# Moving half a filter's rearranging copies from GpSimd to ScalarE in a fused layer-norm, long-convolution and gated-MLP kernel, under a new written-out order

## The chip, the cores and the metric

The kernel runs on one core of a Trainium2 chip. Its engines work side by side, each through its own instructions in the order in which they were written: TensorE (PE in the profile) multiplies matrices, VectorE (DVE), ScalarE (ACT) and GpSimd (POOL) work on tiles in the on-chip memory, and SyncE (SP) mostly starts DMA transfers. An engine that waits for a semaphore holds up everything behind it in its queue. The metric is the time of one execution on the device, in microseconds; lower is better.

## The reference, cut to what matters

```python
xn = layernorm(q)                                  # q: 2048 x 512, bf16
# branch A
k_shift = sum of 4 shifted copies of k, each times one column of shift_k
kv = k_shift * v
y = irfft(rfft(kv, 4096) * rfft(ssm_k, 4096))[:2048] + kv * ssm_D    # per channel
s = xn * y
# branch B: w_gate and w_up are 512 x 1792, w_down is 1792 x 512
h = gelu(xn @ w_gate) * (xn @ w_up)
g = silu(h @ w_down)
out = q + s * g
```

Branch A is a causal convolution along 2048 positions with a filter `ssm_k` (512 channels of 2048 taps each) for each channel. Branch B is a gated MLP. Both take the same normalised input.

## The kernel before, in words

The sequence of 2048 positions lies on 128 partitions with 16 positions each. It is worked in four quarters (q = 0 to 3) of 512 positions. For a quarter the MLP has 14 units (m = 0 to 13): four matmuls against `Wg`, four against `Wu` (each 128x512 out of a 128x128 weight block), a GELU on ScalarE that reads the first result out of PSUM into `GE` (L1137), and a multiplication on VectorE of the second result with `GE` into `HT` (L1140). The first two units of quarter 0 are done in halves of 256 columns (L1128, L1130). After that come the down projections against `Wd`, 14 matmuls for each of four tiles.

The convolution is a Fourier transform in two stages, written as matmuls. The shifted sum of k is made on VectorE in four groups of 2048 elements per partition: `KAC` is the running sum, `KTM` a product (L1005, L1009, L1011), and a last multiplication by v overwrites `V` (L1013). Its four columns of `shift_k` are first copied out by GpSimd into `SKB` (L986). The first stage multiplies data by the table `F1`, the results are evicted from PSUM, stored to a scratch in HBM (`ZH` for the filter, `ZK` for the data), read back in another order (`BH`, `BK`), and go through the second stage as 16 small 32x32 matmuls against `TF`. The spectra are multiplied on VectorE (`HS` and its row-swapped copy `HW`, both by `KB`), the way back uses `MI`, `ZI` and `G1`.

The filter must be transposed before its first stage, since channels lie on its partitions. It comes in four pieces `Hn[0..3]` of 128 channels (512 KB each). Pieces 0 and 1 are transposed by TensorE (L878) and copied out of PSUM into `HTr`. Pieces 2 and 3 go another way: four copies `h_perm` (tasks 58 to 61, L894), two for each piece, lay them out in `HP`, so that the taps of one residue stand together, and two transposing DMAs `h_dtr` on SP's queue (tasks 62 and 63, L899) turn `HP` into `HTD`. The first `HTD` matmuls are called the J stage (tasks `ps1J`), those of `HTr` the H stage.

Nothing is scheduled at run time. The program is a list of 788 tasks. The string `SEQ` gives the order in which they are emitted, so it gives each engine its order; a `b` behind a number picks the task's second engine. `Sched.run` goes through `SEQ` and reckons times with the costs written at each task; those costs only choose which PSUM bank and which buffer a task gets (`pF` of MLP results holds at most four banks). The constants `LOAD_NS`, `ISSUE` and `LANDS` are such reckoning too. All loads from HBM are on SP's queue in the order of `SEQ`, whatever `ORDER` says.

What a matmul of the MLP must wait for is thus: the weights' load, the transposed input `xnT`, and the bank, which is free when the GELU or the multiplication that read its last content is done.

Of the kernel before, what the change touches and what calls it, by code (L numbers as in the profile page):

```python
# [16 lines left out]
NT = 16  # L17
# [7 lines left out]
N_WARM = 11  # L25
ORDER = "x01 h0 x11 h1 x22 w0 w1 h2 h3 D0 w2 s0 k0 v0 x1 w3 k1 v1 d0 d1 k2 v2 k3 v3 x2 x3"
SEQ = (
    "0 2 17 19 5 18 21 1 3 8 4 9 10 11 6 22 12 13 7 66 67 68 74 51 50 69 75 83 53 87 70 76 103 77 71 23 20 24 72 73 84 88 37 113 108 78 118 109 "
    "378 79 380 379 80 81 381 85 104 370 86 55 89 90 371 372 54 56 14 390 392 15 373 119 25 458 32 456 29 459 382 457 30 384 33 114 57 454 398 "
    "374 28 383 460 31 35 455 385 376 391 394 461 462 34 52 396 393 16 395 400 399 149 375 26 147 464 397 120 115 116 148 466 40 463 38 401 402 "  # L30
    "377 110 64 150 406 465 404 468 39 470 407 27 60 117 121 403 151 111 405 410 386 36 469 82 408 152 58 409 473 387 388 153 414 472 474 105 412 "
    "467 122 389 47 59 430 106 422 415 154 62 416 471 411 159 417 61 155 63 44 100 413 432 156 42 43 426 94 107 112 101 41 427 428 423 429 157 "
    "424 475 431 91 425 95 477 499 92 433 93 160 158 161 97 476 96 418 503 420 504 98 505 478 500 162 231 506 163 501 226 232 227 491 185 102 502 "
    "419 507 228 233 99 508 509 234 519 229 521 144 164 421 165 65 515 123 493 46 124 167 510 520 479 45 168 145 444 135 445 522 517 129 169 166 "
    "481 170 146 138 136 446 130 480 235 241 171 141 482 139 483 447 172 175 125 173 176 137 434 242 140 142 236 132 449 230 450 237 126 174 133 "
    "177 238 178 485 127 239 451 243 131 143 448 184 484 134 246 244 435 183 248 247 128 240 48 251 179 180 181 249 436 245 439 182 437 440 49 "
    "253 252 254 441 486 452 487 261 442 438 489 516 262 453 263 443 250 643 264 488 256 644 492 186 255 258 191 511 257 259 518 495 645 187 265 "
    "490 647 497 512 494 513 496 641 188 642 260 527 196 648 266 523 646 649 551 189 190 279 498 652 514 650 653 192 651 206 529 524 193 552 194 "
    "528 531 197 530 292 536 198b 525 532 546 199 267 547 555 654 557 558 556 201 553 526 268 537 271b 533 280 541 284 281 554 559 542 269 270 "
    "272 273 548 534 560 293 538 563 297 561 543 562 539 544 294b 549 200 274 535 663 540 195 664 564 277b 545 278 550 675 665 666 677 683 295 "  # L40
    "275 685 276 655 684 296 657 282 703 676 686 202 678 283 671 298 285 659 299 331 656 673 305 203 658 204 211 286 705 661 660 662 318 672 609 "
    "287 288b 290 610 597 300 611 674 599 598 301b 612 303 593 306 310b 595 581 307 205 600 304 582 569 583 207 308 302 208 584 216 601 309 594 "
    "209 596 617 571 319 311 320b 704 706 619 602 291 323 570 212 603 213 312 618 604 214 572 210 585 586 587 725 313 289 357 577 620 314 215 "
    "316b 717 613 321 332 578 344 579 615 221 691 336b 333 317 580 315 614 217 693 692 322 218 616 219 565 324 566 325 588 326 567 220 568 667 "
    "327b 668 329 694 334 335 669 345 699 349 346 687 573 701 222 670 337 347 348 689 575 223 328 589 224 688 574 330 605 350 338 690 225 351 607 "
    "358 606 700 576 362b 679 359 339 591 608 707 702 590 342 340b 352 709 360 361 341 621 631 592 353 622 343 355 363 364 681 356 365 721 680 "
    "354 713 632 633 636 366 367 637 368b 682 369 638 719 626 627 723 639 634 715 635 623 640 624 628 695 720 629 748 625 724 755 733 731 630 722 "
    "716 727 726 697 782 696 708 711 718 749 710 698 728 732 750 735 751 729 730 778 734 712 741 786 738 714 756 776 742 736 777 784 743 737 739 "
    "744 780 745 752 746 787 757 785 758 779 781 762 763 753 754 764 747 769 765 740 770 783 759 760 761 766 767 771 772 773 768 774 775 "
)  # L50
NF_BANKS = 4
ISSUE = 470.0
LOAD_NS = {("x0_", 262144): 1200.0, ("x0_", 131072): 450.0, 262144: 900.0, 524288: 1350.0, ("x", 524288): 2100.0, ("h", 524288): 1300.0, ("wg", 524288): 1550.0, ("wu", 524288): 1450.0, 917504: 2620.0, ("sk", 524288): 1500.0, 344064: 1250.0, 46080: 350.0, 3072: 100.0, 1024: 200.0}
W_XT, W_SW, W_BK, W_BH, W_ZI, W_BI, W_ZK, W_MI, W_G1 = 1665000, 600000, 555000, 703000, 333000, 640000, 490000, 740000, 222000
NC_PAIRS = 4
SMALL = 1.15 * 262144
# [235 lines left out]
class Sched:  # L292
# [8 lines left out]
    FIRST = {"loads": 1050.0, "SP": 30500.0}  # L301
    DRAIN = 121.0
    EARLY, TAKEN, SHARED, WAIT = (0.0, 1.0), 1400.0, 46000.0, 3300.0
    LANDS = ()

    def __init__(self):
        self.tasks = []
# [37 lines left out]
    def run(self):  # L345
# [5 lines left out]
        for name in SEQ.split():  # L351
# [13 lines left out]
            if eng == "loads":  # L365
                free[eng] = t.start + dur * (self.EARLY[1] if t.start < self.EARLY[0] else 1.0)
                if n_loads < len(self.LANDS):
                    free[eng] = self.LANDS[n_loads] - self.LOAD_LAT
                n_loads += 1
# [21 lines left out]
def act(n, sb=False):  # L391
    return 170.0 + n * 0.833 + (30.0 if sb else 0.0)


def dve(n, rate):
    return 150.0 + n / 0.96 / rate


def build_kernel(nc, A_q, A_k, A_v, A_shift_k, A_ssm_k, A_ssm_D, B_w_gate, B_w_up, B_w_down, out):
    with ExitStack() as es0:  # L400
# [8 lines left out]
        def at(name, shape, dt, offset):  # L409
            return nc.alloc_sbuf_tensor_at(name, shape, dt, offset=offset)  # L410
# [46 lines left out]
        Hn = at("Hn", [128, KD, S_LEN], BF16, g_at)  # L457
        HTr = at("HTr", [128, NT // 2, DM], BF16, kk_at - 16384)
        HP = at("HP", [128, NT, 2, 128], BF16, kk_at - 8192)
# [45 lines left out]
        S = Sched()  # L505
        res = trk.res

        def dsem(name):
            return DSem(nc.alloc_semaphore(name), name)
# [79 lines left out]
        def dma(eng, out_ap, in_ap, sem, r, w):  # L589
            trk.dma(eng, lambda e: e.dma_start(out=out_ap, in_=in_ap), sem, r=r, w=w)  # L590
# [3 lines left out]
        def load(name, out_ap, in_ap, w_res, w_buf, nbytes, ring="SP", r=(), rb=()):  # L594
            sem = dsem("d_" + name)
            ns = LOAD_NS.get((name.rstrip("0123456789"), nbytes)) or LOAD_NS[nbytes]
            last_load[0] = S.add([("loads", ns)], lambda e: dma(ring, out_ap, in_ap, sem, r, w_res), r=rb, w=w_buf, nbytes=nbytes)

        def op(engs, fn, r=(), w=(), rr=(), ww=(), lat=0.0, after=()):

            def emit(e):
                R = rr() if callable(rr) else rr
                W = ww() if callable(ww) else ww
                trk.op(e, lambda h: fn(e, h), r=R, w=W)
            return S.add(engs, emit, r=r, w=w, lat=lat, after=after)

        def copy(e, h, o, i, scale=1.0):
            if e == "ACT":
                return h.activation(o, i, ACTF.Copy, scale=scale)  # L609
            if scale != 1.0:  # L610
                return h.tensor_scalar(o, i, scale, None, ALU.mult)
            return h.tensor_copy(o, i)  # L612
# [21 lines left out]
        bHP, bHTD = [[B(f"{x}{h}") for h in range(2)] for x in ("HP", "HTD")]  # L634
# [255 lines left out]
        h_perm, h_dtr = [], []  # L890
        d_htd = [dsem(f"d_htd{hf}") for hf in range(2)]
        for hf in range(2):
            for k in range(2):
                h_perm.append(op([("POOL", 1250.0)], lambda e, h, hf=hf, k=k: h.tensor_copy(HP[:, 8 * hf:8 * hf + 8, k, :], Hn[:, 2 + k, :].rearrange("p (a t) -> p t a", t=NT)[:, 8 * hf:8 * hf + 8, :]),  # L894
                                 r=[bHn[2 + k]], w=[bHP[hf]], rr=[R_Hn[2 + k]], ww=[R_HP[hf]]))
        for hf in range(2):
            def dtr(e, hf=hf):
                o = HTD[:, 8 * hf:8 * hf + 8, :, :].rearrange("p t k d -> p (t k) d")
                trk.dma("SP", lambda h: h.dma_start(out=o, in_=HP[:, 8 * hf:8 * hf + 8, :, :].rearrange("p t k a -> p (t k a)"), transpose=True), d_htd[hf], r=[R_HP[hf]], w=[R_HTD[hf]])  # L899
            h_dtr.append(S.add([("loads", 4500.0)], dtr, r=[bHP[hf]], w=[bHTD[hf]], nbytes=W_XT))  # L900
        HT0 = HTr[0:1, 0, :].rearrange("p (d c) -> p c d", c=2)[:, 0, :]
        HD0 = HTD[0:1, 0, :, :].rearrange("p k d -> p (k d)")
        bFold, bFoldD = B("fold"), B("foldD")
# [1 line left out]
           r=[bHD, *[bHTr[k][0] for k in range(2)]], w=[bFold], rr=[R_D, *R_HTr[0]], ww=R_HTr[0])  # L905
        op([("DVE", 420.0)], lambda e, h: h.tensor_tensor(HD0, HD0, Drow[:, 256:512], ALU.add),
           r=[bHD, bHTD[0]], w=[bFoldD], rr=[R_D, R_HTD[0]], ww=[R_HTD[0]])
# [284 lines left out]
        for j in range(8):  # L1192
            p = B(f"psy{j}", pC)
# [29 lines left out]
        for j in range(6):  # L1223
            d_out.append(dsem(f"d_out{j}"))
            g = G[:, 2 * j:2 * j + 2, :].rearrange("p t d -> p (t d)")
            x = X[:, 2 * j:2 * j + 2, :].rearrange("p t d -> p (t d)")
# [4 lines left out]
                  r=[b2], w=[B(f"out{j}")], nbytes=262144)  # L1231
# [55 lines left out]
```

## Time and profile before

| | us |
|---|---|
| median of 3 runs | 201.49 |
| lowest, highest | 201.22, 202.07 |
| the profiled execution, on the device | 202.13 |
| its span, first to last instruction | 200.3 |
| PE busy | 190.8 |
| DVE busy | 165.8 |
| ACT busy | 119.2 |
| POOL busy | 24.5 |

The profiled execution lies 0.64 us above the median of the runs, and 1.83 us of it lie outside the span. Matmuls overlap in the array, and their ends are modelled, so "PE busy" tells when there was a matmul under way, not that the array worked at its full rate; the rate is seen from the distance of one matmul to the next, 0.219 us for one of 512 columns at full clock (49 of them in 10.74 us). DVE instructions overlap as well: the next one starts some 0.07 us ahead of the listed end of the last.

### The profile page before, as it was taken

What the parts mean: (1) busy time and instruction counts of PE and PEld (TensorE: products, weight loads), DVE (VectorE), ACT (ScalarE), POOL (GpSimd) and SP (SyncE); (2) the same over time, 40 slices, a digit from 0 to 9 for tenths busy, and PEclk for the clock granted to TensorE, in tenths of its full rate; (3) what the DMA queues carried; (4) which work ended last, traced back from release to release, by engine and by line L of the source; (5) the groups of instructions that cost most, each with busy time, mean ns of one, the idle gap of its engine ahead of it and who ended that gap; (6) DMA issues with size and microseconds to landing.
All of it is one profiled execution on the core that took longest, in us unless ns stands there. A gap on an engine that the chain in (4) does not pass through costs nothing.

```text
span 200.3 us, 3498 instructions
## 1 busy us (share of the span) xinstructions
PE 190.8 (95%) x1365; PEld 85.7 (43%) x1377; DVE 165.8 (83%) x244; ACT 119.2 (60%) x167; POOL 24.5 (12%) x36
## 2 busy tenths in 40 slices
PE   8899988499999999999999999999999999999994
PEld 2575543134444444443434443333434334444442
DVE  7699799969988999866978787887989793288994
ACT  5787993236688786987345666677668562340121
POOL 5502699100000000020030000000000000000000
PEclk9999999669999999999999999999999999999999
DMA  5999997999967869998999993387922235866374
GB/s 172 321 340 341 387 407 225 208 253 330 252 203 253 279 164 264 411 380 238 363 154 337 252 315 127 106 279 243 318 112 105 108 124 193 303 218 211 105 265 157
DMA packets 46102, 49.19 MB, mean 246 GB/s; under 512 B 12803, under 2 KB 39943, under 8 KB 46086
## 3 DMA queue, kind: packets, MB, share of 16 engines
q1 hardware_dynamic: 37510, 42.67, 69.0%
q10 hardware_dynamic: 8576, 6.29, 9.8%
q8 instruction: 11, 0.18, 0.4%
q14 instruction: 5, 0.04, 0.1%
HBM read 27.39 MB, written 14.68 MB: 210 GB/s over the span
## 4 chain that ended last, share of the span: by engine, by line
PE 79%; DVE 7%; SPq 5%; DMA 4%; issue 3%; ACT 0%; DVEq 0%
PE psall L618 74%; SPq L590 5%; PE psall L1028 5%; DMA KK<-in_A_k_dram 4%; DVE KAC L1005 2%; DVE KTM L1009 2%; DVE KAC L1011 1%; DVE HT L1140 1%; DVE G L1175 0%; DVE G L1174 0%; ACT G L1172 0%; DVE HTr L904 0%; DVE HT L1130 0%; DVE XN L835 0%; DVEq L173 0%
## 5 line engine op out<-in xcount | busy, mean ns | idle before, releaser
L618 PE MATMUL psall<-xnT,Wu 128*128 128x512 bf16 (+1 forms) x232 | 57.5, 382 | 0.0
L618 PE MATMUL psall<-xnT,Wg 128*128 128x512 bf16 (+1 forms) x232 | 56.5, 377 | 0.0
L618 PE MATMUL psall<-Wd,HT 128*128 128x512 bf16 (+2 forms) x229 | 50.9, 366 | 0.7 <-issue 0.3
L1140 DVE TENSOR_TENSOR HT<-psall,GE 128x512 bf16<-128x512 f32 x54 | 36.6, 683 | 10.5 <-PE psall L618 10.2
L1137 ACT ACTIVATE GE<-psall 128x512 bf16<-128x512 f32 x54 | 31.5, 602 | 23.1 <-PE psall L618 14.6
L618 PEld LDWEIGHTS psall<-xnT,Wu 128*128 128x128 bf16 x232 | 22.3, 100 | 27.2 <-issue 5.0
L618 PEld LDWEIGHTS psall<-Wd,HT 128*128 128x128 bf16 x238 | 22.4, 98 | 26.0 <-issue 1.3
L618 PEld LDWEIGHTS psall<-xnT,Wg 128*128 128x128 bf16 x232 | 22.0, 99 | 26.4 <-issue 3.2
L1009 DVE TENSOR_TENSOR KTM<-KK,SKB 128x2048 bf16<-128x2048 bf16 x12 | 17.6, 1470 | 0.1
L609 ACT ACTIVATE HS<-psall 128x1024 bf16<-128x1024 f32 x15 | 14.6, 1030 | 3.0 <-PE psall L1028 3.0
L609 ACT ACTIVATE X<-psall 128x1024 bf16<-128x1024 f32 (+1 forms) x17 | 13.8, 825 | 4.2 <-PE psall L618 4.2
L1011 DVE TENSOR_TENSOR KAC<-KAC,KTM 128x2048 bf16<-128x2048 bf16 x12 | 15.8, 1320 | 0.1
L609 ACT ACTIVATE AST<-psall 128x1024 bf16<-128x1024 f32 x12 | 12.1, 1022 | 3.8 <-PE psall L618 3.8
L609 ACT ACTIVATE KB<-psall 128x1024 bf16<-128x1024 f32 x10 | 10.0, 1020 | 6.7 <-PE psall L1028 6.7
L1166 DVE SCALAR_TENSOR_TENSOR G<-G,psall 128x512 bf16<-128x512 bf16 x12 | 7.8, 681 | 7.1 <-ACT G L1164 7.1
L609 ACT ACTIVATE BO<-psall 128x1024 bf16<-128x1024 f32 x9 | 9.1, 1023 | 6.9 <-PE psall L1028 6.9
L1172 ACT ACTIVATE G<-psall 128x512 bf16<-128x512 f32 (+2 forms) x5 | 2.6, 512 | 16.6 <-PE psall L618 16.6
L612 DVE CAST BO<-psall 128x1024 bf16<-128x1024 f32 x7 | 8.6, 1223 | 4.5 <-PE psall L1028 4.5
L1164 ACT ACTIVATE G<-psall 128x512 bf16<-128x512 f32 x12 | 6.8, 597 | 8.5 <-PE psall L618 8.4
L821 DVE BATCH_NORM_STATS2 stats<-X 128x6 f32<-128x512 bf16 x16 | 10.6, 676 | 1.2 <-DMA X<-in_A_q_dram 1.2
L1091 DVE TENSOR_TENSOR HW<-KB,HW 128x1024 bf16<-128x1024 bf16 x16 | 10.9, 682 | 0.0
L831 POOL TENSOR_SCALAR mv<-mv 128x1 f32<-128x1 f32 (+1 forms) x7 | 2.0, 281 | 72.6 <-DVE mv L822 72.6
(82 smaller groups left out, 189.3 us busy)
## 6 DMA issues: line engine op xcount, KB each, us to landing
BH<-ZH SPq DMA_DIRECT2D x8, 512.0 KB, 5.2
BK<-ZK SPq DMA_DIRECT2D x8, 512.0 KB, 6.1
HW<-HS SPq DMA_DIRECT2D x16, 256.0 KB, 3.0
ZI<-BO ACTq DMA_DIRECT2D x16, 256.0 KB, 2.5
BI<-ZI SPq DMA_DIRECT2D x8, 512.0 KB, 4.3
ZK<-AST SPq DMA_DIRECT2D x6, 512.0 KB, 3.7
Hn<-in_A_ssm_k_dram SPq DMA_DIRECT2D x4, 512.0 KB, 8.4
KK<-in_A_k_dram SPq DMA_DIRECT2D x4, 512.0 KB, 9.6
```

The lines of the kernel that those rows point to most:

```text
L590: trk.dma(eng, lambda e: e.dma_start(out=out_ap, in_=in_ap), sem, r=r, w=w)
L609: return h.activation(o, i, ACTF.Copy, scale=scale)
L612: return h.tensor_copy(o, i)
L618: return h.matmul(o, lhsT=l, rhs=r, start=st, stop=sp)
L821: t_stats[t] = op([("DVE", 670.0)], lambda e, h, t=t: h.bn_stats(stats[:, t, :], X[:, t, :]), r=[bX[q][t % 4]], w=[bst[t]], rr=[R_X[t]], w ...
L1009: op([("DVE", dur)], lambda e, h, j=j, m=m: h.tensor_tensor(KTM[:, m.slot, :, :], kk(j), sk(j), ALU.mult), r=need + [bSKB[j], a], w=[m], r ...
L1011: op([("DVE", dur)], lambda e, h, m=m: h.tensor_tensor(KAC[:, a.slot, :, :], KAC[:, a.slot, :, :], KTM[:, m.slot, :, :], ALU.add), r=[m], ...
L1028: trk.op("PE", lambda h: h.matmul(ps(s, i)[b, :], lhsT=wt(col)[a, :], rhs=data(col)[a, :], start=n < 16, stop=n >= len(todo) - 16, tile_po ...
L1091: return hd.tensor_tensor(o, flat(KB, kb[h]), o, ALU.mult)
L1137: op([("ACT", act(512))], lambda e, h: h.activation(GE[:, g.slot, :], bank(pg), ACTF.Gelu_apprx_tanh), r=[pg], w=[g], rr=lambda: R_bank(pg ...
L1140: op([("DVE", dve(512, 1))], lambda e, h: h.tensor_tensor(HT[:, q % 2, m, :], bank(pu), GE[:, g.slot, :], ALU.mult), r=[pu, g], w=[bHT[q][m]],
L1166: op([("DVE", dve(512, 1))], lambda e, h, g=g, pc=pc: h.scalar_tensor_tensor(out=g, in0=g, scalar=1.0, in1=pc(), op0=ALU.add, op1=ALU.mult ...
```

## The change

The four `h_perm` copies may run on ScalarE (or VectorE) instead of GpSimd, and the new `SEQ` takes ScalarE for all four. `copy` on ScalarE is an ACTIVATE with the function Copy. Two of the costs that the reckoning uses change (`LOAD_NS` of the first pieces of x, `h_dtr`), and `LANDS` gives it landing times of the first three loads; none of these adds an instruction. The new `SEQ` moves nearly everything a little. What stands out:

- SP's queue: the filter's piece 1 is issued ahead of the first weights, piece 2 six places earlier, the second 512 KB pieces of `Wg` and `Wu` later (behind piece 2 and, for `Wu`, behind `SKR` and the first 512 KB of k), the third pieces of the weights a little earlier. The two transposing DMAs stay behind the loads of v, but one load of k is now ahead of them.
- One of the four evictions into `HTr` goes from ScalarE to VectorE (task 57b).
- The four ScalarE instructions that turn the sign of `TF` (L729, task 82) come later, behind the GELU of quarter 1's unit 7.
- Later on, SP has the loads `BK` of quarter 0 of the spectrum behind the first `HW` transfers, where they were ahead of them.

```diff
 SEQ = (
-    "0 2 17 19 5 18 21 1 3 8 4 9 10 11 6 22 12 13 7 66 67 68 74 51 50 69 75 83 53 87 70 76 103 77 71 23 20 24 72 73 84 88 37 113 108 78 118 109 "
...
+    "17 19 18 0 3 1 2 4 8 5 7 11 21 6 9 51 12 66 67 68 74 20 69 76 75 50 10 77 13 53 22 83 23 84 87 118 70 108 71 72 113 55 73 88 78 79 54 370 52 "
+    "109 37 57b 80 85 372 110 89 81 371 15 86 373 24 32 90 111 379 378 114 28 374 380 382 384 376 14 454 456 458 381 25 459 375 460 26 455 119 "
...
-LOAD_NS = {("x0_", 262144): 1200.0, ("x0_", 131072): 450.0, 262144: 900.0, 524288: 1350.0, ("x", 524288): 2100.0, ("h", 524288): 1300.0, ("wg", 524288): 1550.0, ("wu", 524288): 1450.0, 917504: 2620.0, ("sk", 524288): 1500.0, 344064: 1250.0, 46080: 350.0, 3072: 100.0, 1024: 200.0}
+LOAD_NS = {("x0_", 262144): 1400.0, ("x0_", 131072): 450.0, 262144: 900.0, 524288: 1350.0, ("x", 524288): 2100.0, ("h", 524288): 1300.0, ("wg", 524288): 1550.0, ("wu", 524288): 1450.0, 917504: 2620.0, ("sk", 524288): 1500.0, 344064: 1250.0, 46080: 350.0, 3072: 100.0, 1024: 200.0}
...
-    LANDS = ()
+    LANDS = (3150.0, 3490.0, 5770.0)
...
-                h_perm.append(op([("POOL", 1250.0)], lambda e, h, hf=hf, k=k: h.tensor_copy(HP[:, 8 * hf:8 * hf + 8, k, :], Hn[:, 2 + k, :].rearrange("p (a t) -> p t a", t=NT)[:, 8 * hf:8 * hf + 8, :]),
+                h_perm.append(op([("ACT", act(1024, True)), ("DVE", dve(1024, 1))], lambda e, h, hf=hf, k=k: copy(e, h, HP[:, 8 * hf:8 * hf + 8, k, :], Hn[:, 2 + k, :].rearrange("p (a t) -> p t a", t=NT)[:, 8 * hf:8 * hf + 8, :]),
...
-            h_dtr.append(S.add([("loads", 4500.0)], dtr, r=[bHP[hf]], w=[bHTD[hf]], nbytes=W_XT))
+            h_dtr.append(S.add([("loads", 3600.0)], dtr, r=[bHP[hf]], w=[bHTD[hf]], nbytes=W_XT))
```

## The prediction, made before the changed kernel ran

> **What bounds the kernel now.** I read the page's slices first, then the table by stage for 24 to 52 us, then the timelines of the engines that stop there, and last the waits. In the slices PE is at nine tenths nearly throughout, with one hole in slices 7 to 9, where the granted clock falls to six tenths as well; DVE is full there, and POOL is busy just ahead.
>
> ```profile
> PE   8899988499999999999999999999999999999994
> DVE  7699799969988999866978787887989793288994
> ACT  5787993236688786987345666677668562340121
> POOL 5502699100000000020030000000000000000000
> PEclk9999999669999999999999999999999999999999
> ```
>
> The stage table gives, for each stretch, PE, PE's weight loads, DVE, ACT and POOL busy, the granted clock and the DMA share. From 28 to 44 us PE issued 46 matmuls, half of what the stretches beside it did:
>
> ```profile
> 24.00:28.00 4.00, 4.00 (x23) 1.87 (x21) 4.00 (x4) 3.69 (x7) 4.00 (x3) 1.00 1.10 384
> 28.00:32.00 4.00, 3.33 (x19) 1.51 (x19) 4.00 (x5) 2.42 (x6) 3.77 (x2) 1.00 0.90 343
> 32.00:36.00 4.00, 2.19 (x10) 0.80 (x9) 4.00 (x2) 1.35 (x2) 3.88 (x2) 1.00 0.88 206
> 36.00:40.00 4.00, 2.38 (x6) 0.93 (x7) 4.00 (x5) 1.26 (x3) 0.00 (x0) 0.60 1.11 204
> 40.00:44.00 4.00, 4.00 (x11) 1.45 (x10) 2.77 (x4) 1.44 (x2) 0.00 (x0) 0.54 0.90 220
> ```
>
> The timelines of PE, DVE and POOL (start, length, what; in brackets the wait) name the cause:
>
> ```profile
> 24.93 5.02 POOL L894 COPY HP<-Hn 128x1024 bf16<-128x1024 bf16 x2
> 25.02 3.03 DVE L1009 TENSOR_TENSOR KTM<-KK,SKB 128x2048 bf16<-128x2048 bf16 x1
> 27.97 0.68 DVE L1140 TENSOR_TENSOR HT<-psall,GE 128x512 bf16<-128x512 f32 x1
> 28.57 2.46 DVE L1011 TENSOR_TENSOR KAC<-KAC,KTM 128x2048 bf16<-128x2048 bf16 x1
> 30.17 5.71 POOL L894 COPY HP<-Hn 128x1024 bf16<-128x1024 bf16 x2 [0.23 <-DMA Hn<-in_A_ssm_k_dram]
> 31.56 2.45 DVE L1009 TENSOR_TENSOR KTM<-KK,SKB 128x2048 bf16<-128x2048 bf16 x1
> 33.93 3.03 DVE L1005 TENSOR_TENSOR KAC<-KK,SKB 128x2048 bf16<-128x2048 bf16 x1
> 37.49 1.21 DVE L1011 TENSOR_TENSOR KAC<-KAC,KTM 128x2048 bf16<-128x2048 bf16 x1
> 37.62 0.61 PE L618 MATMUL psall<-HTr,F 128*128 128x512 bf16 x1 [3.38 <-DVE HT L1140]
> 38.03 3.62 PE L618 MATMUL psall<-xnT,Wu 128*128 128x512 bf16 x8
> ```
>
> Four 2048-wide VectorE operations between two on-chip tiles take 2.45 to 3.03 us while the four `HP` copies run on POOL; the first one behind them takes 1.21. The multiplication `HT`, which reads PSUM, keeps its 0.68. PE waits 3.38 us for an `HT` that is queued behind the 3.03 us `KAC`. Then eight matmuls take 3.4 us, 0.425 each in place of 0.219: the half clock.
>
> What the hole costs: from 25.70 to 50.52 us PE does 76 matmuls of 512 columns (0.219 us each, from the chain's 49 in 10.74: 16.6), two of 256 (0.2) and eight transposes (0.7), 17.5 us of work in 24.8. So 7.3 us are lost: 3.4 by the long wait, some 2.7 by 13 matmuls at half clock, the rest by short waits (0.67, 0.49) at full clock. From 5.9 to 24 us the same count gives 18.6 us of work in 18.1, so nothing is lost ahead of it, and from 50 us on the chain is almost solid PE up to 196.6. What shortens the end is what closes this hole.
>
> **The change part by part.**
>
> *Copies off POOL.* DVE's excess is 1.82 + 1.25 + 1.24 + 1.82 = 6.1 us. It goes as far as POOL causes it; bounds 0 (the loads of that time cause it, DMA share 0.88 to 1.10) and 6.1. I take 6.1, as at 36 to 40 us, with the DMA share at 1.11, the operations are back at 1.21. `SKB`'s copies stay on POOL, and so does the 0.29 of the first `KAC` (1.50). The Trainium skill, page "SBUF — State Buffer", section "SBUF: two separate sides", says that VectorE with two SBUF inputs and a GpSimd instruction that reads SBUF exclude each other for the whole instruction, and ScalarE has a port of its own. The rows agree, and the sum by that rule is the same 6.1.
>
> *Copies on ACT.* No row shows this form on ACT. The nearest are 1.02 to 1.05 (128x1024 out of PSUM, L609) and 0.786 for 512 strided elements on chip (L729) against 0.60 for 512 out of PSUM; with that surcharge 1.23. I take 1.2, 4.8 in all; the ends are 4.1 and, by POOL's fastest copy (2.04), 8.2. Against that, 3.1 us of L729 leave the same stretch for about 44 us, and one `HTr` eviction (1.05) goes to DVE (bounds 0.68 and the 1.22 of L612). So ACT has little more to do from 17 to 40 us, but its order counts: each copy stands ahead of GELUs.
>
> *Loads.* By bytes issued, 512 KB land each 1.4 us. Piece 1 lands at 8.8 instead of 10.0, first weights at 9.4 and 10.0 instead of 8.0 and 8.8; I had TensorE transpose piece 1 meanwhile and count 0.6 us lost. Piece 2 lands at 17.4 (24.0 before), piece 3 at 28.7 (30.0). The second `Wu` piece has 1.5 MB more ahead of it: 24.0 instead of 19.25.
>
> *A walk through the new order* with these rows (PE 0.865 per four matmuls, DVE 0.61 for `HT` and 1.15 to 1.2 for a shift operation, as they follow one another): the gate matmuls with the second `Wg` piece start at 14.5; the second `Wu` piece is first needed at 25.3 (landed by 24.0); the copies run on ACT at about 18.5, 23, 30 and 34.5, of which the third waits for piece 3 at most a little; each bank is free 0.3 to 2 us ahead of its next matmul. So PE runs through, and what it had done at 50.3 is done at 44.1: 6.2 us gained. DVE has the same 12 of its 32 shift operations done at 43.5, so it doesn't fall behind.
>
> *What is late next.* (a) From 44 to 55 us ACT has L729's 3.1 us, the stores it issues (0.4 each) and six evictions of 1.02 nearly back to back; by the walk the J matmuls find their PSUM pair taken three times, 0.3 to 0.5 us each, about 1.1 us (bounds 0 and 2.5). (b) `BK`: before, the last `ZK` store was issued at 87.02, landed 3.5 later, `BK` was issued at 90.57, landed 5.3 later at 95.9, and its matmuls ran at 97.8, 1.9 in hand. Now the last first-stage matmul of the data comes 0.7 nearer to that use, and `BK` is issued behind two `HW` transfers which wait for the eviction of `HS` (1.0 more and 1.2 of issue). Of the 1.9 in hand nothing is left; PE is 0 to 2.4 us late, and I take 0.6. Other steps keep slack: `BH` about 4 us, the `xnT` transposes 1.5 or more.
>
> Sum: 6.2 - 1.1 - 0.6 = 4.5 us off the profiled 202.13, 197.6; the median lies 0.64 below the profiled run, hence 197.0.
>
> *Short waits and the clock.* The clock stayed at 1.00 with waits of 0.67 and 0.49 at 28 to 32 us and fell behind one of 3.38. The Trainium skill, "TensorE: Matmul & The Clock Gate", section "What's actually happening", gives one idle window of about 3.4 us, with which this agrees. Its section "A second HAM failure mode: psum-queue depth-cycling" speaks against this change: many micro-waits for PSUM can make the clock oscillate. That rule here is the third rival.
>
> **The rivals.**
>
> 1. *ACT becomes the bound; slower.* A copy reads 32-byte steps, and on POOL it took 2.04 to 3.04 us. If it is the pattern that is slow, four copies cost up to 2.7 each on ACT, 1.5 more than taken; ACT is full from 15 to 40 us, so these 6 us reach the GELUs and through the banks PE: 197.0 + 6 = 203.0. It decides from 2.6 us per copy on. For it: no row has this form. Against: `HTr` evictions with scattered writes took 1.05, and POOL's copies shared their time with DVE.
>
> 2. *The second `Wu` piece comes late; slower too.* The queue held one issue for 5.53 us before (16.33). If that befalls this load and it lands at 30, PE waits 4.7 and pays 2.7 of half clock: 204.4. It takes until 28.3 or so to eat the gain. Against: the held issue had 8.5 MB issued ahead of it, this one 6.5.
>
> 3. *Short waits pull the clock down* from 47 to 56 us: nine us at half rate cost 4.5, 201.5, no change. Against: 28 to 32 us at 1.00.
>
> 4. *Half a gain.* Both waits (a) and (b) at their upper ends, or a third of DVE's excess staying: 197.0 + 2.3 = 199.3.
>
> 5. *No price for (a) and (b)*, and the new order packed better elsewhere: under 195.
>
> **How the numbers follow.** Forecast 197.0, with 195.0 to 198.5 for it: 0.60. Half a gain (198.5 to 200.5): 0.14. Under 195: 0.03. No change, the clock rival and part of the others: 0.07. ACT as the bound 0.09, `Wu` late 0.07. A change of 0.5%, 1.0 us, is about what a measurement tells from none. Faster: 0.60 + 0.14 + 0.03 = 0.77; same 0.07; slower 0.16. Leaving out the 0.03 below and most of the 0.16 above gives 195.0 to 201.5.
>
> **What would show it.** Right: no copy on POOL, every shift operation of DVE near 1.21 but the first; no PE wait over 1 us from 24 to 50; the granted clock 1.00 in all slices; `HP` copies on ACT near 1.2; solid PE chain from before 20 us. (a) shows as waits of PE for ACT's evictions at 47 to 55, (b) as a wait of the `BK` matmuls for a DMA near 91. Wrong: `HP` copies over 2 us, a wait for `Wu`, a new slice with a lowered clock, or slow shift operations without POOL.

## The result, and the profile after

| | us | runs |
|---|---|---|
| before, on the same chip | 201.78 (201.22 to 202.62) | 4 |
| after | 196.0 (195.77 to 196.51) | 4 |
| ratio | 0.9724, 95% interval 0.968 to 0.9767 | |
| the profiled execution of after | 195.77, span 194.0 | 1 |

The change made the kernel 2.8% faster; 197.0 was forecast, with 195.0 to 201.5 around it. In the page's slices of after, the hole of PE in slices 7 to 9 is gone and no slice has a lowered clock:

```profile
PE   7799999999998999999999999999999999999993
DVE  7599699998999993977788789878897963588993
ACT  6787999979876978868648767756577531222121
POOL 6412420000000000020300000000000000000000
PEclk9999999999999999999999999999999999999999
```

The stage table of after (PE, weight loads, DVE, ACT, POOL busy, granted clock, DMA share, GB/s) has PE busy throughout from 24 to 44 us, with 109 instructions in five stretches where before had 69. The DMA share is 1.00 to 1.08 there (before: 0.88 to 1.11):

```profile
24.00:28.00 4.00, 4.00 (x21) 1.76 (x19) 3.57 (x5) 4.00 (x6) 1.58 (x1) 1.00 1.08 398
28.00:32.00 4.00, 4.00 (x26) 2.08 (x25) 4.00 (x5) 3.61 (x5) 0.00 (x0) 1.00 1.01 386
32.00:36.00 4.00, 3.95 (x21) 1.89 (x20) 4.00 (x6) 4.00 (x6) 0.00 (x0) 1.00 1.01 190
36.00:40.00 4.00, 4.00 (x20) 1.84 (x19) 4.00 (x6) 4.00 (x8) 0.00 (x0) 1.00 1.06 204
40.00:44.00 4.00, 4.00 (x21) 1.80 (x19) 3.93 (x5) 2.73 (x5) 0.00 (x0) 1.00 1.00 238
```

The timelines of DVE and ACT in after (start, length, what; in brackets the wait) show what became of the two sides of the change:

```profile
23.65 1.42 DVE L1005 TENSOR_TENSOR KAC<-KK,SKB 128x2048 bf16<-128x2048 bf16 x1 [0.30 <-DMA KK<-in_A_k_dram]
25.62 1.23 DVE L1009 TENSOR_TENSOR KTM<-KK,SKB 128x2048 bf16<-128x2048 bf16 x1
...
19.01 2.08 ACT L609 ACTIVATE HP<-Hn 128x1024 bf16<-128x1024 bf16 x1 [0.62 <-DMA Hn<-in_A_ssm_k_dram]
```

The shift operations of DVE are back at 1.22 us, so the 6.1 us of excess are gone. The copies cost ACT 2.1 us each, where 1.2 was forecast. When after starts the first matmul of the data's first stage (44.82 us) it has worked through as many matmul columns as before has at 52.03: it is about 7.2 us ahead. (That matmul itself comes only 5.7 us earlier, at 44.82 for 50.52, since the order around it differs.) At the end of the last matmul of all after is 6.4 us ahead (196.6 against 190.2). About one microsecond is given back, most of it at 58 to 63 us, which the end of the experiments takes up.

Three things changed together: the engine of the copies, the order of all the work, and the order of the loads. In the theory of the prediction the copies on POOL slow DVE, DVE keeps PE waiting, and the long wait costs a second time through the clock. The rival readings are that the new order alone brought it, and that the move of engine alone would have done.

### The profile page after: what moved, and what is told of

Read it like the earlier page. It is cut to its first block, busy times and chain, and to the rows that moved or that the text cites. A ratio compares the mean times of both kernels' runs of the same rounds, so it can differ in the third digit from the quotient of the medians.

```text
span 194.0 us, 3492 instructions
## 1 busy us (share of the span) xinstructions
PE 187.5 (97%) x1364; PEld 85.0 (44%) x1377; DVE 159.8 (82%) x245; ACT 125.5 (65%) x170; POOL 14.0 (7%) x32
## 4 chain that ended last, share of the span: by engine, by line
PE 87%; DMA 7%; ACT 2%; issue 1%; SPq 1%; DVE 1%
PE psall L618 80%; PE psall L1028 5%; DMA Hn<-in_A_ssm_k_dram 3%; DMA ZH<-X 3%; SPq L590 1%; PE psall L854 1%; ACT G L609 1%; PE psall L878 1%; ACT X L609 1%; ACT ASX L609 0%; ACT GE L1137 0%; DVE G L1175 0%; DVE G L1174 0%; ACT G L1172 0%
## 5 line engine op out<-in xcount | busy, mean ns | idle before, releaser
L618 PE MATMUL psall<-xnT,Wu 128*128 128x512 bf16 (+1 forms) x232 | 55.8, 372 | 0.0
L618 PE MATMUL psall<-xnT,Wg 128*128 128x512 bf16 (+1 forms) x232 | 55.3, 372 | 0.0
L618 PEld LDWEIGHTS psall<-xnT,Wu 128*128 128x128 bf16 x232 | 21.6, 98 | 25.9 <-issue 3.8
L609 ACT ACTIVATE X<-psall 128x1024 bf16<-128x1024 f32 (+1 forms) x18 | 15.1, 846 | 3.8 <-DMA ZH<-X 3.3
L609 ACT ACTIVATE HS<-psall 128x1024 bf16<-128x1024 f32 x14 | 13.7, 1022 | 4.2 <-PE psall L1028 4.2
L1011 DVE TENSOR_TENSOR KAC<-KAC,KTM 128x2048 bf16<-128x2048 bf16 x12 | 14.6, 1218 | 0.1
L1009 DVE TENSOR_TENSOR KTM<-KK,SKB 128x2048 bf16<-128x2048 bf16 x12 | 14.6, 1217 | 0.0
L821 DVE BATCH_NORM_STATS2 stats<-X 128x6 f32<-128x512 bf16 x16 | 10.3, 677 | 3.9 <-DMA X<-in_A_q_dram 3.9
L609 ACT ACTIVATE KB<-psall 128x1024 bf16<-128x1024 f32 x11 | 11.0, 1021 | 3.6 <-PE psall L1028 3.6
L1091 DVE TENSOR_TENSOR HS<-KB,HS 128x1024 bf16<-128x1024 bf16 x16 | 10.8, 682 | 0.0
L618 PE MATMUL psall<-V,F 128*128 128x512 bf16 x30 | 8.8, 379 | 0.4 <-ACT ASX L609 0.3
```

What stands on the lines that cost most here:

```text
L618: return h.matmul(o, lhsT=l, rhs=r, start=st, stop=sp)
L821: t_stats[t] = op([("DVE", 670.0)], lambda e, h, t=t: h.bn_stats(stats[:, t, :], X[:, t, :]), r=[bX[q][t % 4]], w=[bst[t]], rr=[R_X[t]], w ...
L1009: op([("DVE", dur)], lambda e, h, j=j, m=m: h.tensor_tensor(KTM[:, m.slot, :, :], kk(j), sk(j), ALU.mult), r=need + [bSKB[j], a], w=[m], r ...
L1011: op([("DVE", dur)], lambda e, h, m=m: h.tensor_tensor(KAC[:, a.slot, :, :], KAC[:, a.slot, :, :], KTM[:, m.slot, :, :], ALU.add), r=[m], ...
L1091: return hd.tensor_tensor(o, flat(KB, kb[h]), o, ALU.mult)
```

## The experiments

Each kernel below keeps the task list, and with it the choice of banks and buffers, of the kernel it starts from.

### The engine and the order apart

The old order with the copies on ACT (an edit of before):

```diff
-                h_perm.append(op([("POOL", 1250.0)], lambda e, h, hf=hf, k=k: h.tensor_copy(HP[...], Hn[...]),
+                h_perm.append(op([("POOL", 1250.0)], lambda e, h, hf=hf, k=k: copy(e, h, HP[...], Hn[...]),
...
-            t.emit(t.eng)
+            t.emit("ACT" if t in h_perm else t.eng)
```

> The order of before, every task and bank the same; only the four HP copies go to ScalarE at the places in the order where GpSimd had them. Theory (the copies on GpSimd slow VectorE's shift operations, and this makes the hole): the shift operations take 1.22 us all through and the 3.4 us wait for HT goes; ScalarE pays 4 x 2.08, and its first copy stands where it must wait for the filter's piece 2 (landed at 24.0, ScalarE is there at 21.5), so part of the 7.3 us comes back as waits for ScalarE: 198.5 us, between 196.5 and 200. Rival (the gain is the new order's): 201.5 or slower.

Measured: 203.2 us (202.97 to 203.68), ratio 1.0114 (1.0055 to 1.0173). It was to be faster, and it is slower. The timelines of DVE, ACT and PE in this kernel:

```profile
25.45 1.23 DVE L1009 TENSOR_TENSOR KTM<-KK,SKB 128x2048 bf16<-128x2048 bf16 x1
30.97 0.69 DVE L1140 TENSOR_TENSOR HT<-psall,GE 128x512 bf16<-128x512 f32 x1 [4.29 <-ACT GE L1137]
...
24.56 2.08 ACT L609 ACTIVATE HP<-Hn 128x1024 bf16<-128x1024 bf16 x1 [2.81 <-DMA Hn<-in_A_ssm_k_dram]
27.50 1.58 ACT L729 ACTIVATE TFA<-TF 128x512 bf16<-128x512 bf16 x2
...
30.37 0.57 ACT L1137 ACTIVATE GE<-psall 128x512 bf16<-128x512 f32 x1
...
27.18 1.04 PE L618 MATMUL psall<-xnT,Wg 128*128 128x512 bf16 x4 [1.94 <-ACT X L609]
30.99 1.04 PE L618 MATMUL psall<-xnT,Wg 128*128 128x512 bf16 x4 [1.68 <-ACT GE L1137]
```

Two things are to be read here. With the loads and the order of before, and only POOL relieved, the shift operations take 1.22 to 1.23 us (the first 1.48): so POOL's copies were what slowed them, and the bound of zero (that the loads did it) falls: the DMA share at 24 to 32 us is 1.02 to 1.08 here. But the time doesn't follow. ACT stands 2.81 us at its first copy until filter piece 2 has landed, then does the copy, two evictions, L729's 3.1 us, and only then a GELU at 30.37, for which DVE's `HT` waits 4.29 and, through the bank, PE. PE is busy 12.9 us of the 20 from 24 to 44. The wait was handed from DVE to ACT; in the new order piece 2 is loaded earlier and L729 comes behind this stretch. Neither of these two was changed alone, so how much each is worth stays open.

The new order with the copies still on POOL (an edit of after):

```diff
-            t.emit(t.eng)
+            t.emit("POOL" if t in h_perm else t.eng)
```

> The new order, every task and bank the same; only the four HP copies go back to GpSimd. Theory: three of the copies now fall on shift operations of VectorE (25 to 36 us), three or four of these take 2.4 to 3.0 us instead of 1.22, some 4.5 us, of which PE's reserve of banks hides 1 to 1.5: 199.5 us, between 198 and 201.5. Rival (the order alone gives the gain): 196.0, with PE solid from 14 us on.

Measured: 198.31 us (197.37 to 199.15), ratio 0.987 (0.9788 to 0.9952), at the lower end of what was expected. The order alone brings about half of the gain. Its stage table at 36 to 40 us, its four copies (shortest, median, longest in ns; first and last start in us), the row of the waits of PE's weight loads for DVE's `HT` (sum, times, longest, in us), and two lines of DVE's timeline show why:

```profile
36.00:40.00 4.00, 2.87 (x13) 1.01 (x12) 4.00 (x5) 2.07 (x5) 0.00 (x0) 1.00 1.06 210
```

```profile
L612 POOL COPY HP<-Hn x4: 2260/2781/3036, 18.4 to 32.7; 128x1024 bf16<-128x1024 bf16 x4
```

```profile
PEld psall L618 <- DVE HT L1140: 4.3, 7, 1.2
```

```profile
18.31 2.46 DVE L835 TENSOR_SCALAR XN<-X,mv 128x512 bf16<-128x512 bf16 x2
27.88 1.23 DVE L1009 TENSOR_TENSOR KTM<-KK,SKB 128x2048 bf16<-128x2048 bf16 x1 [1.92 <-POOL SKB L986]
```

The copies start at 18.4 instead of 24.9 us, the first before DVE has a shift operation to do; two operations are slow (2.47 and 2.45) and one a little (1.62), 2.9 us of excess instead of 6.1. That is not all that POOL costs here: while the first copy runs (18.36 to 20.62) two normalising operations `XN` take 2.46 us together, where after's take 0.72, and the second copy stands ahead of POOL's last `SKB`, for which DVE waits 1.92. What is left comes to PE as seven waits of at most 1.2 us, at 36 to 40 above all, and the clock stays at 1.00. The four corners:

| | old order | new order |
|---|---|---|
| copies on POOL | 201.1 (before) | 198.3 |
| copies on ACT | 203.2 | 196.0 (after) |

The same move of engine costs 2.1 us in the one order and saves 2.3 in the other (the intervals of the two ratios in the right column don't meet). Neither rival reading holds alone; the parts don't add.

### The clock's share of the hole

Before, with PE kept at work during the long wait: twelve more matmuls of the same kind, into the same place, ahead of the one that is behind the wait.

```diff
-                        trk.op("PE", lambda h, c=c: mm(h, ps(s, c), F1[:, c, :], data, True, True), ...)
+                        for _ in range(13 if (x, u, c) == ("H", 1, 0) else 1):
+                            trk.op("PE", lambda h, c=c: mm(h, ps(s, c), F1[:, c, :], data, True, True), ...)
```

> The kernel before, but the first HTr matmul of the task that has the 3.38 us wait is done 13 times instead of once (it writes the same result into the same bank), 2.6 us of work inside the wait. Theory (the wait makes the clock fall): the granted clock stays at 1.00 from 36 to 44 us and 1.7 to 2.7 us of the half-clock loss come back, VectorE being the next limit there: 199.4 us. Rival (the clock falls for another reason, or VectorE sets the pace after the wait whatever the clock): 201.5, no change.

Measured: 199.75 us (199.13 to 200.2), ratio 0.9956 (0.9924 to 0.9989). PE's timeline of this kernel behind the dummies, which end at 36.8, and its stage table:

```profile
37.57 0.39 PE L618 MATMUL psall<-HTr,F 128*128 128x512 bf16 x1 [0.82 <-DVE HT L1141]
37.80 1.89 PE L618 MATMUL psall<-xnT,Wu 128*128 128x512 bf16 x8
```

```profile
40.00:44.00 4.00, 4.00 (x20) 1.81 (x19) 4.00 (x6) 2.41 (x3) 0.00 (x0) 1.00 0.83 229
```

The real work is no earlier (37.57, against 37.62 in before), but the eight matmuls behind it take 1.89 us instead of 3.62, and the clock at 40 to 44 is 1.00 instead of 0.54. So it was PE's idleness that lowered the clock, and work that nobody needs covers it: the rival (no change) falls. The gain is 1.4 us by the medians (0.9 by the ratio), under the 2.7 that the prediction counted for the half clock, yet 3.0 between the two profiled executions (202.13 and 199.13). Before's own executions tell why. Beside these experiments it was timed 54 times, with the mean granted clock (the share of its full speed that TensorE was allowed) of each execution:

| mean clock of before | executions | us |
|---|---|---|
| 0.983 | 8 | 202.0 to 202.6 |
| 0.989 to 0.991 | 40 | 200.3 to 202.2 |
| 0.998 to 1.000 | 6 | 199.0 to 200.0 |

A mean of 0.983 over 200 us is what 6.8 us at half clock give; 0.991 is what 3.6 us give, and 0.989 4.4. Before's profiled execution has 0.983, so the prediction read the hole in its dearest form. The filled wait has 1.00 in all ten executions and runs as those six of before do. By the medians of the three groups (202.4, 201.1, 199.5) the clock costs before 1.6 us in most executions and 2.9 in the dearest. So of the 2.8 us that the new order brings with the copies on POOL, some 1.6 are the clock's, which is at 1.00 in all four executions of that kernel.

### How much ACT can take, and what a copy costs

Each copy done twice on ACT, in after:

```diff
             t.emit(t.eng)
+            if t in h_perm:
+                t.emit(t.eng)
```

> The changed kernel with each HP copy done twice in a row on ScalarE, 8.4 us more of its time from 19 to 38 us. Theory (ScalarE has little in reserve; the prediction's limit was 2.6 us per copy): 4.2 us per copy makes TensorE wait for GELUs and evictions, 200 us, between 198 and 203. Rival (ScalarE has the reserve): under 197.

Measured: 203.18 us (201.9 to 204.03), ratio 1.0095 (1.006 to 1.0129). From the tile `HP` and from the waits of PE's weight loads:

```profile
L609 ACT ACTIVATE HP<-Hn x8: 2037/2079/2123, 19.0 to 41.5; 128x1024 bf16<-128x1024 bf16 x8
```

```profile
PEld psall L618 <- ACT X L609: 6.8, 6, 2.1
PEld psall L618 <- ACT GE L1137: 2.6, 3, 1.8
```

8.3 us more on ACT cost 7.5 us (the difference of the two ratios, 0.0371, of 201.1): nearly all of it reaches PE, by evictions of `X` and by GELUs. So ACT has hardly a reserve beyond what after asks of it. On the other side, a copy that reads 1024 neighbouring elements instead of every sixteenth:

```diff
-  copy(e, h, HP[:, 8 * hf:8 * hf + 8, k, :], Hn[:, 2 + k, :].rearrange("p (a t) -> p t a", t=NT)[:, 8 * hf:8 * hf + 8, :])
+  copy(e, h, HP[:, 8 * hf:8 * hf + 8, k, :], Hn[:, 2 + k, 1024 * hf:1024 * hf + 1024].rearrange("p (t a) -> p t a", a=128))
```

> The changed kernel with HP copies that read 1024 elements side by side instead of one in 16; the filter's channels 256 to 511 are thus laid out wrongly and this part of the computation is left out. Theory (the step of 32 bytes is what makes a copy 2.08 us instead of 1.2): 1.05 to 1.25 us each. Rival (reading on-chip memory costs this on ScalarE whatever the step): 2.08. Both: 196.0 us within 0.5, since TensorE waits for no copy.

Measured: 195.66 us (195.09 to 196.93), ratio 0.9718 (0.9659 to 0.9778), the same as after. And with the step on the other side, neighbouring elements read and every 256th written (both transposing DMAs then wait for all four copies, and the first of them is put directly ahead of the second):

```diff
-  copy(e, h, HP[:, 8 * hf:8 * hf + 8, k, :], Hn[:, 2 + k, :].rearrange("p (a t) -> p t a", t=NT)[:, 8 * hf:8 * hf + 8, :])
+  copy(e, h, HP[:, :, k, 64 * hf:64 * hf + 64].rearrange("p t a -> p a t"), Hn[:, 2 + k, 1024 * hf:1024 * hf + 1024].rearrange("p (a t) -> p a t", t=NT))
```

> The changed kernel with the same rearrangement the other way round: each copy reads 1024 elements side by side and writes them 512 bytes apart, so both transposing DMAs wait for all four copies. Theory (only reads with a step cost): 1.05 to 1.3 us each. Rival (a step costs on the write side as well): 2.08. 196.0 us within 0.5 for both.

Measured: 207.73 us (207.1 to 208.59), ratio 1.0311 (1.0252 to 1.0371). Neither theory had that time, nor the length of a copy. The tile `HP` again, first of the reading variant, then of the writing one:

```profile
L609 ACT ACTIVATE HP<-Hn x4: 1048/1057/1066, 18.3 to 32.5; 128x1024 bf16<-128x1024 bf16 x4
```

```profile
L609 ACT ACTIVATE HP<-Hn x4: 4762/4778/4799, 18.9 to 40.8; 128x1024 bf16<-128x1024 bf16 x4
```

The same 1024 elements per partition take 1.06 us in a row, 2.08 with a read step of 32 bytes and 4.78 with a write step of 512 bytes. The pattern, not the engine or the place, is what doubled the forecast 1.2. The Trainium skill, page "ScalarE: Activation LUTs", section "What ACT_TABLE_LOAD costs", gives 186 ns and 0.833 ns an element for such an instruction, by estimate 1.04 us here. The first row alone agrees with it. Its page "SBUF — State Buffer", section "Door 1: The DMA port swizzle (why `[64,N]` ≈ `[32,N]`)", says that accesses which each go to a new 16-byte line pay a penalty. The second and third row agree in direction; it gives no size for either.

Against the length of a copy the times are 195.7 (1.06), 196.0 (2.08), 203.2 (4.16, as two) and 207.7 (4.78). It is flat up to 2.08 and steep behind it. On a straight line between 2.08 and 4.16, after would be no better than before from about 3.6 us per copy on; the bend itself was not measured. The last point holds more than the length of a copy: there both transposing DMAs wait for all four copies, and the clock falls once (mean 0.992).

### The order of the loads

After with filter piece 1 issued behind the first weights, as it was before:

```diff
+        t = next(x for x in order if x.n == 20)
+        order.remove(t)
+        order.insert(1 + next(i for i, x in enumerate(order) if x.n == 23), t)
```

> The changed kernel with the filter's piece 1 issued behind the first weights again, TensorE's order as it is. Theory (the load order fits the order of TensorE): piece 1 lands some 1.3 us later, TensorE waits for it with nothing else to do, 197.2 us. Rival (the start is not on the path): 196.0.

Measured: 197.24 us (196.7 to 198.21), ratio 0.9802 (0.9758 to 0.9846). In the list of waits, PE stands for the filter once, for 2.1 us:

```profile
PE psall L878 <- DMA Hn<-in_A_ssm_k_dram: 2.1, 1, 2.1
```

In after this wait is 0.8 in two, the longer 0.6, so it has grown by 1.3. The new order of tasks needs piece 1 that early. This part of the change is worth 1.2 us by the medians; the intervals of the two ratios (0.9758 to 0.9846 and, for a repeat of after on the same chip, 0.9682 to 0.9767) just touch.

After with the second piece of `Wu` issued later (the same three lines, task 30 put behind task 27):

> The changed kernel with the second piece of Wu issued behind the filter's piece 3. It landed at 25.4 and was used at 25.6; now it should land near 30. Theory (a wait beyond about 3.4 us halves the clock): TensorE waits 4.4 us and loses 2 to 2.7 more at half clock, 202.5 us. Rival (only the wait is paid): 200.4. Second rival (the loads behind it come earlier and repay it): under 199.

Measured: 202.74 us (201.55 to 204.54), ratio 1.0073 (1.0038 to 1.0108). PE's timeline of this kernel, and the row of the stage table behind the wait:

```profile
29.85 3.20 PE L618 MATMUL psall<-xnT,Wu 128*128 128x512 bf16 x8 [4.94 <-DMA Wu<-in_B_w_up_dram]
```

```profile
30.26:33.68 3.42, 3.42 (x9) 1.18 (x8) 2.29 (x3) 0.00 (x0) 0.00 (x0) 0.50 0.73 269
```

Eight matmuls take 3.20 us after the wait, much as in before after theirs (3.62). So the second rival's mechanism is there. Its price was a little high: 7.4 us forecast for a landing at 30, 6.7 measured (202.74 against 196.0) for one at 29.7. In after its cause did not occur. How near it was is seen in after itself: the matmul in question started at 25.59 without a wait, and the piece had landed at 25.4, 0.2 us ahead. In the profiled execution of a repeat of after (196.02 us, 194.76 to 196.67, ratio 0.9724, 0.9682 to 0.9767) it came too late by 0.9, with the clock at 1.00 and hardly a trace of it in the time:

```profile
25.76 1.89 PE L618 MATMUL psall<-xnT,Wu 128*128 128x512 bf16 x8 [0.93 <-DMA Wu<-in_B_w_up_dram]
```

### The microsecond given back

At 58 to 63 us after's PE waits for evictions, and ACT, which does them, waits for a store. The timelines of ACT and PE's weight loads in after:

```profile
58.28 1.02 ACT L609 ACTIVATE X<-psall 128x1024 bf16<-128x1024 f32 x1 [1.54 <-DMA ZH<-X]
60.29 1.02 ACT L609 ACTIVATE X<-psall 128x1024 bf16<-128x1024 f32 x1 [0.99 <-DMA ZH<-X]
...
61.37 0.11 PEld L618 LDWEIGHTS psall<-HTD,F 128*128 128x128 bf16 x2 [0.69 <-ACT X L609]
62.28 0.11 PEld L618 LDWEIGHTS psall<-V,F 128*128 128x128 bf16 x2 [0.80 <-ACT ASX L609]
```

`X` is the staging tile of the filter's J stage; an eviction can't overwrite it before its last store to `ZH` has left. I held the load of the third quarter of the input, which shares SP's queue with that time, to be what delays the stores, and moved it (task 48, behind task 191):

> The changed kernel with one load moved: quarter 2 of x is issued behind the second BH load instead of between two ZH stores at 52.8 us. ScalarE's J evictions wait 3.3 us in all for ZH stores that free their buffers, and PE waits 0.7 and 0.8 us for these evictions at 61 to 62 us. Theory (this load stands ahead of the stores in the DMA queues): both waits shrink, 195.2 us. Rival (the transposing DMA ahead of the stores holds them): no change, 196.0.

Measured: 195.78 us (194.48 to 196.48), ratio 0.9717 (0.9676 to 0.9758), not to be told from after. So the theory falls, and the time is the one that the rival gave. ACT's timeline at the first eviction of `X` in this kernel:

```profile
59.52 1.94 ACT L609 ACTIVATE X<-psall 128x1024 bf16<-128x1024 f32 x2 [2.79 <-PE psall L618]
```

The profile puts this wait down to PE, but PE's matmuls for it were done at 57.1. What had just come is the `ZH` store that was issued at 53.38 and landed 6.1 us later, at 59.4. So ACT still waits for `ZH`, longer than in after, and PE's weight loads wait 1.4 us for ACT. SP's timeline in after shows what stands ahead of the stores. The length of an issue is the time for which it holds the queue:

```profile
44.16 6.98 SPq L1039 DMA_TRANSPOSE MI<-TFA  x1
52.27 0.43 SPq L590 DMA_DIRECT2D ZH<-X  x1
54.01 0.92 SPq L590 DMA_DIRECT2D ZH<-X  x1
54.98 3.38 SPq L1039 DMA_TRANSPOSE MI<-TFB  x1
```

In the kernel with the load moved the first of these transposing DMAs held the queue for 8.10 us. `MI` is first used at 101 us. Two kernels move these issues behind later stores (tasks 184 and 185 behind 125 and 255), one both, one the second alone:

```diff
+        for n, behind in ((184, 125), (185, 255)):        # the other kernel: ((185, 255),)
+            t = next(x for x in order if x.n == n)
+            order.remove(t)
+            order.insert(1 + next(i for i, x in enumerate(order) if x.n == behind), t)
```

> The kernel after, with the two transposing DMAs into MI (used from 101 us on) issued later on SP's queue: the first, whose issue holds the queue from 44.2 to 51.1 us, behind the ZH store at 67.9, the second, which holds it from 55.0 to 58.4, behind the ZK store at 76.1. Theory now: these holds delay the ZH stores that free X, so ACT's waits for ZH (3.3 in three) fall under 1, PE has no wait for X or ASX from 56 to 64 (PE busy 8.0 there, 7.44 before), and the time is 0.8 to 1.0 lower, 195.1. Rival: the stores are late for the transfers themselves (DMA share 1.05 to 1.17 in these stretches): the waits stay within 0.3 and the time is 196.0. What it could cost: the queue held near 68 or 77, where BH and ZK issues stand behind; then a wait for BH or BK shows and the time is up to 1 above 196.

> The kernel after, with only the second of these transposing DMAs moved (held 55.0 to 58.4, now behind the ZK store at 76.1). If the hold of 7.0 us at 44.2 is what makes the first stores late, ACT's wait of 1.5 at 58.3 stays and only the later ones of 1.0 and 0.8 shrink: about 195.6. If the second hold does it all, this is as fast as with both moved, 195.1. Rival as there: 196.0, the waits unchanged.

Measured: with both moved 195.28 us (194.79 to 196.74), ratio 0.9726 (0.9684 to 0.9768); with the second alone 195.82 (195.14 to 197.06), ratio 0.9753 (0.9714 to 0.9793). The stage tables at 60 to 64 us, of after, then with both moved, then with the second alone:

```profile
60.00:64.00 4.00, 3.49 (x16) 1.24 (x15) 4.00 (x6) 2.90 (x4) 0.00 (x0) 1.00 1.13 360
```

```profile
60.00:64.00 4.00, 4.00 (x19) 1.67 (x18) 4.00 (x5) 3.84 (x5) 0.00 (x0) 1.00 0.69 190
```

```profile
60.00:64.00 4.00, 3.40 (x16) 1.22 (x15) 4.00 (x5) 3.39 (x4) 0.00 (x0) 1.00 0.90 303
```

It is the first of the two, then, with its hold of 7 us, that costs PE its time there: with it moved the stretch is full, and a matmul of the data that after did at 64.89 is done at 64.08, 0.7 more ahead than at 44.7. The hold is only a part of what makes the stores late. The two `ZH` stores are issued at 49.90 and 52.41 instead of 52.27 and 54.01, 2.4 and 1.6 us earlier, but land only 0.7 and 0.8 earlier (57.49 and 59.46), so ACT's waits for them shrink from 3.3 to 1.8 us and not under 1 as expected. The rest lies in the transfers (5.9 to 7.6 us from issue to landing), as the rival had it. With the second alone moved ACT still waits 2.30 us at 58.60, until the store lands at 58.52 (the profile names PE, which was done at 56.6), and the time is after's. The time does not follow with both moved either: by its ratio this kernel is no faster than after. Its timelines of ACT and PE show the gain going at the next store:

```profile
78.51 3.05 ACT L609 ACTIVATE AST<-psall 128x1024 bf16<-128x1024 f32 x3 [0.90 <-DMA ZK<-AST]
79.82 0.38 PE L618 MATMUL psall<-V,F 128*128 128x512 bf16 x1 [0.68 <-ACT AST L609]
```

At 101 us it is 0.2 ahead of after. The microsecond has a place and in part a cause. By these lines taking it would need the data's stores earlier too; that was not tried.

## Why the prediction was right, and where not

- *What bounded the kernel.* Right, with one correction. POOL's copies slow DVE (the old order with ACT shows it with everything else unchanged), DVE holds PE, the idle PE loses its clock (the filled wait shows that). The correction is to the attribution: the part "copies off POOL" was priced as if it gave the 6.1 us by itself. On its own the order gives 2.8 and the move loses 2.1; the gain needs both. The walk through the new order had counted both together, and so its 6.2 us came out near: what before had done at 50.3 after has done at 43.1, for 44.1 forecast, a gain of 7.2. That POOL slows only the shift operations was too narrow: under the new order its copies also hold up `XN` and the last `SKB`. The count ahead of the hole, 18.6 us of work in 18.1, comes out above the time although PE waits 0.5 us there (for `HTr`, at 7.74), so some of its prices are too high.
- *Copies on ACT.* The term that was mis-sized most: 1.2 each forecast, 2.08 measured, 8.35 us in all, just above the upper end of 8.2 and close to POOL's fastest copy, 2.04. I took the surcharge of a smaller step (4 bytes, read and written, L729) for a read step of 32 bytes. By the prediction's own list, a copy over 2 us was to show it wrong. It did no harm, because at this length the copies' time still reaches nobody, as the variant with 1.06 us shows, which is no faster. That this reserve was there is luck: the walk had not worked it out for 2.08.
- *First rival, ACT as the bound.* Its cause was there and its consequence was not, but it is a true mechanism: doubled copies make the kernel slower than before, and so does the old order with ACT. By the straight line above, the gain is gone at 3.6 us per copy; whether the loss begins at 2.6, as forecast, lies between two measured points.
- *Loads.* All came later than forecast, by 0.6 to 1.1 us at first and by 1.4 to 1.6 from piece 2 on: piece 1 at 9.4 (8.8 forecast), the first weights at 10.3 and 11.1 (9.4 and 10.0), piece 2 at 19.0 (17.4), the second `Wu` piece at 25.4 (24.0), piece 3 at 30.1 (28.7). From piece 2 on the cadence held; ahead of it the stream was slower than it said. Piece 1 cost PE 0.6 to 0.9 as forecast; of the slack that the walk gave the `Wu` piece, 1.3, some 0.2 was left.
- *(a) ACT at 44 to 55 us.* The size held (1.1 forecast, about 1 measured), but by luck, since the place and the cause didn't: PE is solid from 44 to 56, L729's 3.1 us run at 42.5 to 45.6 without a wait of PE, and the loss stands at 58 to 63, behind the stores of `X`, which SP's queue and the transfers made late. The walk had followed PE, DVE and ACT through these stretches, not SP.
- *(b) `BK`.* Wrong by its 0.6 in this execution. `BK` was issued at 85.82 and landed at 90.9; its matmuls ran at 91.64 without a wait. The repeat has a wait of 0.4 there. The loss lies within the bounds given, at the lower end.
- *The clock and short waits* (third rival). The clock of after is 1.00 in every slice, and there were hardly waits to test it on. The doubled copies tested it better: six waits of up to 2.1 us and three of up to 1.8, and a mean clock of 0.998 or more in nine of ten executions (0.990 in the tenth). So short waits of this number did not make the clock swing here.
- *Half a gain* (fourth rival). Its 2.3 us is not what its condition gives: both waits at their upper ends come to 3.2, a third of DVE's excess to 2.0. Nothing else hangs on it.
- *The sum.* 6.2 - 1.1 - 0.6 = 4.5 forecast; between the profiled executions it is 6.4. The first term was 1.0 too low, (a) right in size, (b) not paid. The last step, 0.64 off for the median, was wrong too: it took a difference of before's executions for one that after would have. Before's profiled execution had a mean clock of 0.983, most others 0.989 to 0.991. After's clock is 1.00 in all four, and its profiled execution lies 0.23 below its median. So the sum fell short by 1.9 us and the last step put 0.9 of it back by luck. What is left is 197.0 forecast and 196.0 measured.

## What to carry to other kernels

Take a copy off an engine that blocks another only together with an order that gives the new engine room: its input landed before its turn, and long work of no hurry behind the urgent reads of PSUM. Price a copy by its access step, not by its element count; the same size cost 1, 2 or 4.5 times as much, and it is free only until the waits behind it use up the queue's slack. Where a long wait of TensorE can't be removed, filling it keeps the clock and returns a part of the loss. Before you price a hole from one profile, compare that execution's mean clock with the others'.

## What was not expected of the hardware

The write step. A ScalarE copy of 128x1024 bf16 elements on chip took 4.78 us with a write step of 512 bytes against 2.08 with a read step of 32.

The issue of a transposing DMA held SP's queue for 6.98 us behind a run of loads (8.10 in the kernel with the load of x moved), 3.38 at 55.0, and 1.88 where it was moved to 67.5. What sets this length was not tried.

And the clock. It fell after single waits of 3.38 (before) and 4.94 us (`Wu` late). In the profiled execution of the doubled copies it stayed at 1.00 with waits of up to 2.1. In the kernel with the strided write it fell as well, around a wait of only 2.1 us of PE (2.58 of its weight loads) at 29.4 to 31.5. So the length of a wait alone does not tell whether the clock falls. Finer stretches of the stage table tell more. They show the half clock from 32.72 to 36.13 us with the strided write and from 30.26 to 33.68 with `Wu` late, 3.41 us each, and from 36.83 to 43.66 in before, twice that. The stretches of 3.41 us ahead of each fall (strided write, `Wu` late, before), and then one more of `Wu` late, two steps ahead of its fall:

```profile
29.31:32.72 3.41, 1.32 (x7) 0.45 (x7) 0.64 (x2) 3.41 (x5) 0.00 (x0) 1.00 0.83 311
26.85:30.26 3.41, 0.41 (x2) 0.22 (x3) 0.00 (x0) 0.93 (x2) 0.00 (x0) 1.00 1.07 409
33.41:36.83 3.42, 0.83 (x4) 0.19 (x2) 3.42 (x2) 0.81 (x1) 2.47 (x1) 1.00 1.08 226
23.43:26.85 3.42, 1.48 (x7) 0.49 (x5) 2.93 (x3) 3.42 (x5) 1.68 (x2) 1.00 1.08 392
```

PE was busy 39, 12 and 24% of the stretch ahead of a fall. The one with 43% was followed by full clock. These four rows agree with a clock that is set anew every 3.41 us by PE's busy share in the last such stretch, with the limit for a fall between 39 and 43%; four rows are few for a rule. It would also explain why before loses none, one or two such stretches from one execution to the next: the same wait lies in them now one way, now another. That was not shown, since only one execution of before was profiled. The Trainium skill, "TensorE: Matmul & The Clock Gate", section "What's actually happening", has the clock follow the activity in a window of about 3.4 us. The lengths measured here agree with it.
